# Loading K of head 6 and V of head 5 in one transfer each, with one TensorE loop for the V products of head 5, and c and x in four transfers

## The chip, the cores and the metric

The kernel runs on one core of one Trainium2 chip. The metric is the device time of one execution in microseconds (us). A core has five engines that run side by side: TensorE (PE, matrix products; PEld is its weight load), VectorE (DVE), ScalarE (ACT), GpSimd (POOL) and SyncE (SP), which issues most DMA transfers. All transfers of the core share 16 DMA engines.

## What is computed

One token is decoded through an adaptive-layernorm block. The modulation is `silu(c) @ w_mod`, cut into six vectors of 512. The attention has 32 query heads over 8 key/value heads of 32768 cached positions and 128 channels; the caches are nearly all of the bytes.

```python
h = _layernorm(x) * (1 + ca) + sa
q = (h @ wq)                       # 32 heads of 128
p = softmax(q . k * Dh ** -0.5)    # 4 query heads share one k, v
x = x + ga * ((p @ v) @ wo)
h = _layernorm(x) * (1 + cb) + sb
x = x + gb * (relu(h @ w1) @ w2)   # 512 -> 1792 -> 512
```

## The kernel before

**Storage.** K or V of one head is 8 MB: 128 partitions of 256 positions of 128 channels. SBUF holds three such slots (pool `ring`, line 80), taken in turn by: the weights w_mod and wq, K0, K1, V0, K2, V1, K3, V2, K4, V3, K5, V4, K6, V5, K7, V6, V7, and a last slot for wo, w1 and w2. A load can be issued when the last reader of what lay three places earlier in that list is done. So V5 takes the slot of K5, K7 that of V4, V6 that of K6, V7 that of V5, and the last slot is that of K7.

**The stream.** The list `stream` (lines 161 to 168) fixes the order of the transfers, and all of them go through SP (line 154), in that order. K and V come whole (8 MB) for the early heads, and in halves (two of four steps, 4 MB) where `g >= HALVED`, with `HALVED = 5`: K6 and V5 in halves one after the other, then K7 and V6 half by half in turn. V7 comes in three parts, and the second half of K0 in three (lines 136 to 141): nearly all of it, then the last 512 bytes of rows 0 to 110, then those of rows 111 to 127. A reader waits for the transfer that holds its part. Every transfer raises one of eight completion semaphores, given out in turn over all transfers, those of ACT included; a transfer is issued only when the one that used its semaphore before has landed.

**One head.** For head h, DVE turns K within 32x32 blocks in eight pieces (`turn_k`, line 439, 128x2048 each); PE multiplies each piece with the queries in 8 products (`scores`, line 458), 64 for a head. Then `softmax` runs (lines 466 to 510): a maximum on DVE (line 471), two small PE transposes (476, 490), the exponential on ACT (495), a turn of the result on DVE (500), and on PE the sum (506). The products with V of the head before, `pv(g)` with g = h - 1, are 64 matmuls (line 520).

**How the order around the change is set.** PE and DVE run in the order in which the program is written (`manual_schedule`, lines 633 to 792). For g from 0 to 5 it is: scores of head g + 1; if `g >= HALVED`, `pv(g, (0, 1))`; the softmax of head g + 1; the rest of `pv(g)`, with the sum of the softmax behind it. So for head 5, 32 of the 64 V products are written out ahead of the softmax of head 6 (and run from steps 0 and 1 of V5), and the other 32 behind it. For heads 0 to 4 all 64 stand behind it. The V products behind the softmax are a PE loop (lines 523 to 531) for heads 0 to 5; the 32 ahead of it, and all of heads 6 and 7, are written out. The loop is a critical section: it begins when all that is written before it is done, the exponential of the softmax included. DVE's first operation after a softmax is tied behind the loop's place in the program, and `reciprocal` (line 509), which needs the sum that follows the loop, stands on DVE between the first and the second four turns of the next K (for head 7: between the second and the third).

**The end.** After head 7's scores the last slot's transfers are issued, PE works off the V products of heads 6 and 7, the rows of wo (`project`), the layernorm, w1 (line 761) and w2 (line 784), and DVE closes (789, 791).

**The start.** c and x come by one ACT transfer each into 8 of the 16 partitions of `cx_row` (lines 180 to 182); DVE spreads them (246), and the modulation (322), the first layernorm and the queries (393 to 408) follow.

Of the kernel before, what the change touches and what calls it, by code (L numbers as in the profile page):

```python
# [17 lines left out]
def kernel(  # L18
# [14 lines left out]
    nc = tc.nc  # L33
# [14 lines left out]
    WOROWS = 2  # L48
    LAST = Hkv - 1
    LOOPED = Hkv - 2  # L50
    HALVED = LOOPED - 1
    W2P = [(0, 5), (5, 10), (10, 12), (12, 13), (13, 14)]
    W1P = [(0, KT)]

# [108 lines left out]
    for g in range(LOOPED):  # L163
        stream += [("k", g + 1, s) for s in (halves if g >= HALVED else whole)] + [("v", g, s) for s in (halves if g >= HALVED else whole)]
    for s in halves:
# [5 lines left out]
    def need(key):  # L171
        while key not in loaded:
            load(stream[pos[0]])
            pos[0] += 1
        return loaded[key]
# [3 lines left out]
    wm_sb = need(("wm",))  # L179
    cx_row = const.tile([16, D // 8], BF16)  # L180
    for i, row in enumerate((c[0], A_x[0, 0])):
        nc.scalar.dma_start(out=cx_row[8 * i:8 * i + 8], in_=row.rearrange("(a n) -> a n", a=8))

    ident_bf = const.tile([P, P], BF16)
    make_identity(nc, ident_bf[:])
# [9 lines left out]
    for hp in range(4):  # L195
# [10 lines left out]
        out=mask4, in_=ident_f[:].rearrange("p (x q) -> p q x", q=REP), op=ALU.add, axis=AX.X,  # L206
# [3 lines left out]
    for n in sorted({n * REP for _, n in WOP}):  # L210
        cmask[n] = const.tile([P, P // n], F32, name=f"cmask{n}")
        nc.vector.tensor_reduce(
            out=cmask[n][:], in_=ident_f[:].rearrange("p (c r) -> p c r", r=n), op=ALU.add, axis=AX.X,
# [3 lines left out]
            out=rsel_f[:], in_=ident_f[:].rearrange("p (c r) -> p r c", r=n), op=ALU.add, axis=AX.X,  # L217
# [6 lines left out]
        out=smask[:], in_=ident_f[0:16, 0:16].rearrange("p (s q) -> p s q", q=REP), op=ALU.add, axis=AX.X,  # L224
# [8 lines left out]
        out=place32[:], in_=ident_f[:].rearrange("p (j m) -> p m j", m=32), op=ALU.add, axis=AX.X,  # L233
# [4 lines left out]
        out=rowpick[:, OUT0:OUT1], in_=ident_f[:].rearrange("p (j m) -> p j m", m=32), op=ALU.add, axis=AX.X,  # L238
# [8 lines left out]
        out=cx_bd, in0=cx_row[:].unsqueeze(1).to_broadcast([16, 8, D // 8]),  # L247
# [112 lines left out]
    def four_rows(e, name):  # L360
# [16 lines left out]
        out=nca[:], in0=modT_sb[:, KT:2 * KT], scalar1=-1.0, scalar2=-1.0, op0=ALU.mult, op1=ALU.add,  # L377
# [3 lines left out]
        out=ncb[:], in0=modT_sb[:, 4 * KT:5 * KT], scalar1=-1.0, scalar2=-1.0, op0=ALU.mult, op1=ALU.add,  # L381
# [17 lines left out]
    for i in range(2):  # L399
        nc.vector.transpose(out=q_cols[:, i, :], in_=q_ps[i])  # L400
        nc.scalar.copy(
            out=qT_sb[:, 16 * i:16 * (i + 1)], in_=q_cols[:, i, :].rearrange("p (h r) -> p h r", r=32)[:, :, 0],
# [109 lines left out]
    def pv(g, us, js=range(16)):  # L512

        nb = 4 // len(us)

        PT_g = PT_tiles[g][:].rearrange("p (h j c) -> p h (j c)", h=2, c=32)
        Vs = [need(("v", g, u)) for u in us]

        def step(u, V, PT, Vx):
            nc.tensor.matmul(o_tiles[g][:], lhsT=PT, rhs=Vx, start=False, stop=False, skip_group_check=True)  # L520

        Vf = [V.rearrange("p (s j) d -> p s (j d)", s=4) for V in Vs]
        if g < HALVED or g == HALVED and us[0] > 0:

            with tc.tile_critical() as section:
                last_loop[:] = loop[:] = [section.name]
                with nc.tensor.Fori(0, 512 - 32 * nb + 1, 32 * nb) as at:
                    for b in range(nb):
                        for u, V in zip(us, Vf):
                            step(u, V, PT_g[:, u // 2, 32 * b + 16 * (u % 2):][:, bass.DynSlice(at, 16)],  # L530
                                 V[:, :, Dh * b:][:, :, bass.DynSlice(at * (Dh // 32), Dh)])
        else:
            for u, V in zip(us, Vf):
                for j in js:
                    c0 = 32 * j + 16 * (u % 2)
                    step(u, V, PT_g[:, u // 2, c0:c0 + 16], V[:, :, Dh * j:Dh * (j + 1)])
# [22 lines left out]
    def part_of(g):  # L559
        return [i for i, (g0, n) in enumerate(WOP) if g0 <= g < g0 + n][0]  # L560
# [17 lines left out]
    def spread(i):  # L578

        n = WOP[i][1] * REP  # L580
        o2_ps = small_ps([P, n], "o2_ps")
        nc.tensor.matmul(  # L582
            o2_ps[:], lhsT=oA[i][:].rearrange("p h c -> p (h c)"), rhs=rsel[n][:], start=True, stop=True,
        )
        o2 = const.tile([P, n], BF16, name=f"o2_sb{i}")
        nc.vector.tensor_copy(out=o2[:], in_=o2_ps[:])  # L586
        o2_tiles[i] = o2
# [45 lines left out]
    with tc.manual_schedule(engines={mybir.EngineType.PE, mybir.EngineType.DVE}):  # L633
# [9 lines left out]
        for g in range(LOOPED):  # L643
            h = g + 1
            build_qbd(h)
            for u in range(NTILE):
                for half in range(2):
                    turn_k(h, u, half)
                    scores(h, u, half)
                if soft and u == 1:  # L650
                    next(soft, None)
            if g - 1 in [sum(w) for w in WOP]:
                spread(part_of(g - 2))
            if g >= HALVED:
                pv(g, (0, 1))
            soft = softmax(h)
            next(soft)
            if g > 0:
                blocks(g - 1)
            next(soft)  # L660
            if g > 0:
                o_cols(g - 1)
            next(soft)
            next(soft)
            pv(g, (2, 3) if g >= HALVED else (0, 1, 2, 3))
            if g > 0:
                normalise(g - 1)
            next(soft)
            open_o(h)
            next(soft)  # L670
        g, h = LOOPED, LAST
# [13 lines left out]
        spread(part_of(g - 1))  # L685
        bank_max(h, 0)
        pv(g, (0, 1))
        for u in (2, 3):
            for half in range(2):
# [48 lines left out]
            out=x1T[:], in0=x1T[:], scalar=1.0, in1=xT, op0=ALU.mult, op1=ALU.add, accum_out=stat2[:, 0:1],  # L738
# [31 lines left out]
        for f0, f1 in ((0, FT // 2), (FT // 2, FT)):  # L770
            nc.vector.transpose(out=hidT[:, f0:f1], in_=hid_v[:, f0:f1])
            nc.scalar.activation(
                out=AP(hb.tensor, hb.offset + 32 * f0 + 31, [hb.ap[0], [32, f1 - f0]]),
                in_=hidT[:, f0:f1, 0], func=ACT.Relu,
            )

        for part, (f0, f1) in enumerate(W2P):
            w2_sb = need(("w2", part))
            for ft in range(f0, f1):
                for i in (0, 2, 1, 3):  # L780
                    row = OUT0 + i
# [41 lines left out]
```

## Time and profile before

| what | before |
|---|---|
| median of 3 runs | 354.26 us (354.23 to 354.55) |
| span of the profiled execution | 352.6 us |
| PE busy | 277.9 us, 79% |
| DVE busy | 201.0 us, 57% |
| ACT busy | 25.1 us, 7% |
| read from HBM | 149.42 MB, 424 GB/s over the span |
| granted TensorE clock, mean | 0.937 |

The profile is of one execution. The page gives its span, from the first to the last instruction, and no other time of it; the median of the runs is 1.66 us longer than this span. A page has the busy time of the engines, the span in 40 slices, the DMA queues, the chain of work that ended last, and groups of instructions by source line. The trace behind it can be asked for a timeline: each row is start, duration, engine, line, operation, tiles, count, and in brackets the idle time of the engine before it and what ended that. `DVE Ksb L439 ... <-DMA` means that DVE sat idle until a piece of K had landed. A loop's matmuls stand in one row with their count.

### The profile page before, as it was taken

The numbers are of one execution on the slowest core, as the hardware profiler recorded it, in microseconds if no ns is written. First come the engines' busy times: TensorE is split into PE (matmuls) and PEld (weight loads), VectorE is DVE, ScalarE is ACT, GpSimd is POOL, SyncE is SP. The second block draws the span as 40 slices with busy tenths as digits, with TensorE's granted clock in tenths as the row PEclk, the third lists the DMA queues.
The fourth block names the chain that finished last, engine by engine and source line by source line (L and its number), as shares of the span: only waits on it lengthen the run. The fifth ranks groups of instructions, "written<-read, shape, count | busy, mean of one in ns | idle before, by whom it ended". The sixth has DMA issues, their size and how long they took to land. (4 is left out here: it accounts for less than half of the span.)

```text
span 352.6 us, 3715 instructions
## 1 busy us (share of the span) xinstructions
PE 277.9 (79%) x1310; PEld 113.5 (32%) x1310; DVE 201.0 (57%) x226; ACT 25.1 (7%) x69; POOL 3.1 (1%) x15
## 2 busy tenths in 40 slices
PE   0065891895998599976998499968999799989994
PEld 0021330331333234322333134323444233434442
DVE  6663564984079614974099506975684257744142
ACT  1200103002000200001000200011000100011000
POOL 2000000000000000000000000000000000000000
PEclk9999897798999879998999879996999989999999
DMA  9999989999999999999999999999999999999995
GB/s 357 398 435 452 472 388 461 454 394 454 461 394 448 439 424 439 424 433 439 416 446 446 409 440 461 411 394 454 431 414 435 457 417 420 444 439 409 425 425 214
DMA packets 5224, 149.59 MB, mean 424 GB/s; under 512 B 604, under 2 KB 988, under 8 KB 1628
## 3 DMA queue, kind: packets, MB, share of 16 engines
q1 hardware_dynamic: 5180, 149.43, 98.5%
q8 instruction: 8, 0.13, 0.1%
q14 instruction: 4, 0.03, 0.0%
q10 hardware_dynamic: 32, 0.00, 0.0%
HBM read 149.42 MB, written 0.00 MB: 424 GB/s over the span
## 5 line engine op out<-in xcount | busy, mean ns | idle before, releaser
L439 DVE STREAM_TRANSPOSE Ksb<-Ksb 128x2048 f32<-128x2048 f32 x60 | 133.1, 2276 | 60.2 <-DMA Ksb<-in_A_k_cache_dram 60.2
L520 PE MATMUL o_ps<-Vsb,P_g 128*16 (+1 forms) x512 | 127.0, 408 | 13.0 <-ACT P_g L495 10.0
L458 PE MATMUL S_ps<-Ksb,qbd 128*128 128x512 bf16 x512 | 120.4, 386 | 10.9 <-DVE Ksb L439 9.3
L458 PEld LDWEIGHTS <-qbd 128*128 128x128 bf16 x512 | 49.6, 98 | 78.1 <-issue 21.8
L520 PEld LDWEIGHTS o_ps<-Vsb,P_g 128*16 x352 | 34.0, 97 | 67.8 <-issue 36.5
L520 PEld LDWEIGHTS <-P_g 128*16 128x16 bf16 x160 | 13.8, 90 | 19.0 <-issue 0.4
L420 ACT COPY qbd<-qrep_sb 32x16 bf16<-32x16 bf16 x32 | 6.4, 201 | 175.2 <-PE S_ps L458 174.1
L500 DVE STREAM_TRANSPOSE P_g<-P_g 128x1024 bf16<-128x1024 bf16 x8 | 10.0, 1245 | 14.1 <-ACT P_g L495 14.1
L471 DVE TENSOR_REDUCE m_p<-S_ps 128x1 f32<-128x1024 f32 x7 | 8.6, 1223 | 13.3 <-PE S_ps L458 13.3
L322 PE MATMUL mod_ps<-wmq_sb,siluT 128*1 128x512 bf16 x24 | 3.6, 624 | 9.9 <-DMA wmq_sb<-in_w_mod_dram 9.9
L331 DVE STREAM_TRANSPOSE Ksb<-Ksb 128x2048 f32<-128x2048 f32 x4 | 8.9, 2280 | 1.6 <-DMA Ksb<-in_A_k_cache_dram 1.6
L476 PE MATMUL mT_ps<-ident_f,m_p 128*1 128x128 f32 x8 | 2.2, 270 | 8.9 <-DVE m_p L471 7.9
L495 ACT ACTIVATE P_g<-S_ps,nbias 128x1024 bf16<-128x1024 f32 x8 | 8.9, 1114 | 0.2
L506 PE MATMUL L_ps<-Lexp,ones_f 128*128 128x4 f32 x16 | 3.1, 263 | 6.3 <-DVE Lexp L503 4.3
L492 ACT ACTIVATE nbias<-Mb_ps 128x1 f32<-128x1 f32 x8 | 1.4, 171 | 88.3 <-PE Mb_ps L490 88.3
L509 DVE RECIPROCAL Linv<-L_ps 128x4 f32<-128x4 f32 x8 | 1.3, 164 | 10.9 <-PE L_ps L506 10.9
L252 PE MATMUL xc_ps<-cx_sel,wmq_sb 16*128 16x2 bf16 x4 | 0.3, 172 | 8.7 <-DVE wmq_sb L246 8.7
L555 PE MATMUL acc_ps<-mask_sb,Y 16*128 16x4 f32 x16 | 3.0, 258 | 4.9 <-DVE Y L551 4.9
L548 DVE TENSOR_TENSOR o_ps<-o_ps,smask 16x512 f32<-16x512 f32 x8 | 5.3, 668 | 2.8 <-PE o_ps L520 2.8
L586 DVE CAST o_sb<-o_ps 128x4 bf16<-128x4 f32 (+2 forms) x4 | 0.7, 165 | 10.3 <-PE o_ps L582 10.3
L506 PEld LDWEIGHTS L_ps<-Lexp,ones_f 128*128 128x128 f32 x16 | 2.6, 203 | 9.6 <-issue 5.6
L551 DVE TENSOR_REDUCE Y<-o_ps 16x128 f32<-16x512 f32 x8 | 5.4, 678 | 0.3
(116 smaller groups left out, 82.8 us busy)
## 6 DMA issues: line engine op xcount, KB each, us to landing
Ksb<-in_A_k_cache_dram SPq DMA_DIRECT2D x5, 4096.0 KB, 23.5
Vsb<-in_A_v_cache_dram SPq DMA_DIRECT2D x5, 4096.0 KB, 38.0
wmq_sb<-in_A_wq_dram SPq DMA_DIRECT2D x1, 4096.0 KB, 28.0
Vsb<-in_A_v_cache_dram SPq DMA_DIRECT2D x2, 2048.0 KB, 38.1
Ksb<-in_A_k_cache_dram SPq DMA_DIRECT2D x1, 4032.0 KB, 37.1
wmq_sb<-in_w_mod_dram SPq DMA_DIRECT2D x1, 3072.0 KB, 18.8
tail_sb<-in_A_wo_dram SPq DMA_DIRECT2D x1, 2048.0 KB, 23.0
tail_sb<-in_B_w_dram SPq DMA_DIRECT2D x1, 1792.0 KB, 30.4
```

The costliest lines, as they stand in the source:

```text
L322: nc.tensor.matmul(dst[j // 4][32 * (j % 4):32 * (j % 4) + 1, :], lhsT=src_T[:, kt:kt + 1], rhs=w[:, kt, j * 512:(j + 1) * 512], start=(kt ...
L331: nc.vector.transpose(out=t, in_=t)
L420: nc.scalar.copy(out=o, in_=i)
L439: t = nc.vector.transpose(out=KTt.bitcast(F32), in_=KTt.bitcast(F32))
L458: nc.tensor.matmul(S_ps_tiles[g], lhsT=qbd[g % 2][:, hp, 4 * (7 - s):4 * (7 - s) + P], rhs=KTv[:, 16 * sl:16 * sl + 16, h, :, par], start= ...
L471: behind_loop(nc.vector.reduce_max(out=m_p[:], in_=S_g.rearrange("p g f -> p (g f)"), axis=AX.X))
L495: nc.scalar.activation(out=P_g[:], in_=S_g.rearrange("p g f -> p (g f)"), func=ACT.Exp, bias=nbias[:], scale=scale, accum_out=l_g[:],)
L500: behind_loop(nc.vector.transpose(out=P_g[:], in_=P_g[:]))
L506: nc.tensor.matmul(L_ps[:], lhsT=ones_f[:], rhs=Lexp[:], start=True, stop=True)
L520: nc.tensor.matmul(o_tiles[g][:], lhsT=PT, rhs=Vx, start=False, stop=False, skip_group_check=True)
L548: nc.vector.tensor_tensor(out=o, in0=o, in1=smask[:].unsqueeze(2).to_broadcast([16, 4, Dh]), op=ALU.mult,)
L551: nc.vector.tensor_reduce(out=Y[:], in_=o.rearrange("p s d -> p d s"), op=ALU.add, axis=AX.X)
```

## The change

K of head 6 and V of head 5 are each loaded by one transfer of 8 MB in place of two of 4 MB; the order of the bytes stays. All 64 V products of head 5 are one PE loop behind the softmax of head 6, as for heads 0 to 4. c and x come by two ACT transfers of four partitions each. In the built program the transfers of K7 and of all that follow have the same semaphores as before, since two are added at the start and two are taken away later; 32 matmuls and their 32 weight loads leave the written-out part of PE. After it all line numbers from 183 on are higher by one.

```diff
-    HALVED = LOOPED - 1
+    HALVED = LOOPED
...
     for i, row in enumerate((c[0], A_x[0, 0])):
-        nc.scalar.dma_start(out=cx_row[8 * i:8 * i + 8], in_=row.rearrange("(a n) -> a n", a=8))
+        for a in (8 * i, 8 * i + 4):
+            nc.scalar.dma_start(out=cx_row[a:a + 4], in_=row.rearrange("(a n) -> a n", a=8)[a % 8:a % 8 + 4])
...
-        if g < HALVED or g == HALVED and us[0] > 0:
+        if g < HALVED:
```

## The prediction

> **What bounds the kernel now.** I read the page first: the DMA row, the transfers' total, and the chain that ended last.
>
> ```profile
> DMA  9999989999999999999999999999999999999995
> DMA packets 5224, 149.59 MB, mean 424 GB/s; under 512 B 604, under 2 KB 988, under 8 KB 1628
> DMA 19%; PE 5%; DVE 3%; SPq 0%; issue 0%
> ```
>
> The 16 DMA engines are never idle before the last slice, and the chain ends in transfers. So the stream of bytes sets the end, unless PE comes late to the last weights. The bytes and their order stay, so I ask two things of the change: does the queue run dry anywhere, and how late does PE become? For the first I read SP's timeline, which tells when transfers are issued.
>
> ```profile
> 218.05 0.80 SPq L154 DMA_DIRECT2D Ksb<-in_A_k_cache_dram  x2
> ...
> 256.12 0.33 SPq L154 DMA_DIRECT2D Ksb<-in_A_k_cache_dram  x1
> 270.62 0.33 SPq L154 DMA_DIRECT2D Vsb<-in_A_v_cache_dram  x1
> ...
> 271.46 19.78 SPq L154 DMA_DIRECT2D Vsb<-in_A_v_cache_dram  x4
> 313.02 1.75 SPq L154 DMA_DIRECT2D tail_sb<-in_A_wo_dram  x4
> ```
>
> K6 is issued at 218.05, K7's first half at 256.12, V6's at 270.62; the row from 271.46 ends with the three parts of V7 near 291, and the tail follows at 313.02. For the second I read the timeline of heads 5 and 6, DVE and PE.
>
> ```profile
> 214.63 8.89 DVE L439 STREAM_TRANSPOSE Ksb<-Ksb 128x2048 f32<-128x2048 f32 x4 [12.14 <-DMA Ksb<-in_A_k_cache_dram]
> ...
> 234.35 1.22 DVE L471 TENSOR_REDUCE m_p<-S_ps 128x1 f32<-128x1024 f32 x1 [1.99 <-PE S_ps L458]
> ...
> 239.65 16.31 PE L520 MATMUL o_ps<-Vsb,P_g 128*16 x64 [2.04 <-ACT P_g L495]
> ...
> 243.75 8.89 DVE L439 STREAM_TRANSPOSE Ksb<-Ksb 128x2048 f32<-128x2048 f32 x4 [2.73 <-DMA Ksb<-in_A_k_cache_dram]
> ...
> 256.30 0.36 PE L506 MATMUL L_ps<-Lexp,ones_f 128*128 128x4 f32 x2 [0.34 <-PEq L525]
> ...
> 256.51 14.07 PE L458 MATMUL S_ps<-Ksb,qbd 128*128 128x512 bf16 x64
> ...
> 270.53 7.07 PE L520 MATMUL o_ps<-Vsb,P_g 128*16 128x512 bf16 x32
> 270.75 1.21 DVE L471 TENSOR_REDUCE m_p<-S_ps 128x1 f32<-128x1024 f32 x1
> ...
> 280.74 9.03 PE L520 MATMUL o_ps<-Vsb,P_g 128*16 x32 [2.10 <-DMA Ksb<-in_A_k_cache_dram]
> ...
> 290.10 0.36 PE L506 MATMUL L_ps<-Lexp,ones_f 128*128 128x4 f32 x2 [0.34 <-PEq L525]
> ```
>
> Head 5 is the pattern of a whole K: DVE idles 12.14 us for the landing at 214.6, turns eight pieces, and the maximum starts at 234.35, 19.72 us after the landing. Head 6 is the pattern of halves: DVE starts at 243.75 on the first half, while PE is still in the loop of head 4 that ends at 256.30. So PE does the 64 scores without a wait in 14.07 us, and 32 V products of head 5 (7.07 us) lie over the softmax of head 6.
>
> **The change, part by part.**
>
> *K6 whole.* Its first four pieces must wait for the second half. No row shows that landing, since nobody waits for it; an estimate comes from the rows at 243.75 and at 302.15 (below), where DVE waits for the first half of K6 and the second of K7: six halves in 58.4 us, 9.73 each, so K6 is in at 253.5. By head 5's pattern head 6's maximum then starts at 253.5 + 19.7 = 273.2, plus 0.1 for the small copy that stands before it here: 273.3. Before: 270.75. Queued behind the waiting turn on DVE are the other turns and head 5's reciprocal, whose reader comes much later; the scores wait for the turns. **Term one: 2.5 us.**
>
> *All V products of head 5 behind the softmax.* From the maximum to the loop of 64 takes 239.65 - 234.35 = 5.30 us, from the loop's start to the sum behind it 256.30 - 239.65 = 16.65: 21.95 in all. Before, the same way took 290.10 - 270.75 = 19.35. **Term two: 2.6 us.** The sum of head 6 moves from 290.10 to 273.3 + 21.95 = 295.2, **5.1 us later**. The 64 products may take other times:
>
> ```profile
> 84.24 17.68 PE L520 MATMUL o_ps<-Vsb,P_g 128*16 x64 [2.02 <-ACT P_g L495]
> ```
>
> This loop took 17.68 where that at 239.65 took 16.31, so up to 1.4 more; twice the written-out 7.07 gives 14.1, so up to 2.2 less. I take the nearest, the loop just before.
>
> *The way to the end.*
>
> ```profile
> 298.57 7.07 PE L520 MATMUL o_ps<-Vsb,P_g 128*16 128x512 bf16 x32
> 298.76 0.68 DVE L464 TENSOR_REDUCE m<-S_ps 128x1 f32<-128x512 f32 x1
> 302.15 8.89 DVE L439 STREAM_TRANSPOSE Ksb<-Ksb 128x2048 f32<-128x2048 f32 x4 [2.70 <-DMA Ksb<-in_A_k_cache_dram]
> 305.58 7.41 PE L458 MATMUL S_ps<-Ksb,qbd 128*128 128x512 bf16 x32
> ...
> 332.70 3.62 PE L520 MATMUL o_ps<-Vsb,P_g 128*16 128x512 bf16 x16
> ...
> 336.02 1.16 PE L595 MATMUL end_ps<-tail_sb,o_sb 128*1 128x512 bf16 x16
> ...
> 343.70 0.22 DVE L305 SCALAR_TENSOR_TENSOR h2T<-cen_ln,rstd_ln,modT_sb 128x4 bf16<-128x4 f32 x1
> ...
> 345.30 0.93 PE L761 MATMUL hid_ps<-tail_sb,h2T 128*1 128x448 bf16 x16 [1.28 <-DMA tail_sb<-in_B_w_dram]
> ...
> 347.07 0.73 PE L784 MATMUL end_ps<-tail_sb 128*32 128x128 bf16 x20
> 348.32 1.58 PE L784 MATMUL end_ps<-tail_sb 128*32 128x128 bf16 x36 [0.52 <-DMA tail_sb<-in_B_w_dram]
> ```
>
> The V products at 298.57 stand 8.47 us behind the sum and wait for nothing of the stream, so they start at 303.7. DVE's maximum at 298.76 moves to 303.9, and the last four turns, which began with the landing at 302.15, begin at 304.5 and end at 313.4. PE comes to those scores at 303.7 + 7.0 = 310.7 and does all 32 in 7.1, to 317.8; its last eight start near 316, after the turns. Before they ended at 312.99. **PE is 4.8 us late at the end of the scores**, since 0.3 us of its waiting for DVE goes.
>
> From there PE had no pause for a transfer before 336, where the first rows of wo came as the V products ended (332.70 + 3.62 = 336.32), so the 4.8 us stay. They meet three waits for the stream: 1.28 us ahead of w1 (345.30), 0.52 ahead of w2's second piece (348.32), and, in the last 36 products, what they take beyond the pace of the 20 before them, 1.58 - 36 x 0.73/20 = 0.27. The lateness eats **2.1 us**. What is late next is PE alone; the layernorm's result, ready at 343.92, sets the start of w1 in place of the transfer. **4.8 - 2.1 = 2.7 us later.**
>
> *The queue.* V6's first half, issued at the end of head 6's scores, moves from 270.62 to about 273.2; K7's first half, issued at 256.12 as before, feeds the engines until 253.5 + 3 x 9.73 = 282.7, which leaves 9 us. V7 moves from near 290 to 295.2, and is due when six halves behind K6 (V5, K7, V6) are in, at 311.9: 17 us. The tail moves from 313.02 to 317.8, due after V7 at 331: 13 us. So these moves cost nothing; with cover gone, each would cost its own 2.6 to 5.1 us. The queue behind the issuing SP holds only these transfers in this order. The two saved issues are 0.4 us of SP each (0.80 for two at 218.05), while it has nothing else to do.
>
> *Boundaries.* The Trainium skill's page "DMA: Bandwidth & Descriptors" (Anatomy of one DMA) gives each transfer about 2.0 us beside its bytes, which speaks for this change. The rows here have it hidden behind the next transfer: half a V or K takes 9.73, and two are 19.46. Head 4's and head 5's K, with one whole V between, land at
>
> ```profile
> 176.10 8.89 DVE L439 STREAM_TRANSPOSE Ksb<-Ksb 128x2048 f32<-128x2048 f32 x4 [12.24 <-DMA Ksb<-in_A_k_cache_dram]
> ```
>
> and 214.63, so 19.27 for a whole one. I take 0 for a boundary, the bounds being 0 and 0.2 us.
>
> *c and x, and the start.*
>
> ```profile
> 2.12 20.99 SPq L154 DMA_DIRECT2D Ksb<-in_A_k_cache_dram  x4
> 7.99 0.68 DVE L246 TENSOR_TENSOR wmq_sb<-cx_row,pick 16x512 bf16<-16x512 bf16 x1 [1.82 <-DMA cx_row<-in_A_x_dram]
> 12.76 8.89 DVE L331 STREAM_TRANSPOSE Ksb<-Ksb 128x2048 f32<-128x2048 f32 x4 [1.63 <-DMA Ksb<-in_A_k_cache_dram]
> 20.05 3.58 PE L322 MATMUL mod_ps<-wmq_sb,siluT 128*1 128x512 bf16 x24 [9.86 <-DMA wmq_sb<-in_w_mod_dram]
> 35.10 0.35 SPq L154 DMA_DIRECT2D Vsb<-in_A_v_cache_dram  x1
> 60.18 6.70 DVE L439 STREAM_TRANSPOSE Ksb<-Ksb 128x2048 f32<-128x2048 f32 x3 [0.62 <-DMA Ksb<-in_A_k_cache_dram]
> ```
>
> x was there at 7.99. Two more small transfers add between nothing and twice that, to 24. PE's first large work waits 9.86 us for w_mod anyway; beyond that, V0's issue at 35.10 could slip by 25 us until K1 is in at 60.18. Two semaphores fewer at the start make K0's last small piece wait for K0's first landing, near 12.7, and K1 queues behind it on SP; K1's bytes come last in a queue that lasts until about 41 (60.18 less a whole transfer). Zero for both, and each later head starts anew at its own landing (12.14 us of DVE idle at 214.63).
>
> **Sum.** The profiled execution has a span of 352.6 us; the median of the runs, 354.26, is 1.66 more, which I take for what lies around the span. 352.6 + 2.7 + 1.66 = **357.0 us**, 0.8% slower. A measurement of this kernel can tell about 0.2%, 0.7 us, from no change.
>
> **The rivals.**
>
> *Only one of the two terms arises* (8%): if head 6's scores did not wait for the whole K, or the softmax were covered otherwise, PE would be 2.2 to 2.3 us late against 2.1 of cover: +0.2, **354.4**, no change. Against it: one transfer has one landing that everyone waits for, and the loop at 239.65 began only behind ACT's exponential, as its bracket says.
>
> *The stream shortens* (5%, the other side): each removed boundary saves b, so K6 lands b earlier and the stream ends 2b earlier. The end moves by the later of 2.7 - b (PE) and -2b (stream): faster from b = 2.7 us on, below 351. The 0.2 us above speaks against it. I give b above 2.7 us 3%, and a b of some 2 us, with PE's lateness still deciding, 2%. By the figure of the page "DMA: Bandwidth & Descriptors" of the Trainium skill, 2.0 us for b, the end would move by +0.7, to 355.0; no row here shows it.
>
> *A slow loop* (10%): PE idles ahead of the 64 products, and they run like those at 84.24: +1.4, **358.4**. The loop of head 4 at 239.65, behind the same pause, did not.
>
> **How the numbers follow.** Forecast 77%: 356 to 358. The range reaches from 355.5 (cover larger by half, or the loop shorter by 1.5) to 358.6 (slow loop, landing 0.2 later). Below it lie the rivals of one term and of the shorter stream, 13% together; the sign follows: slower 0.89 (forecast, slow loop, small b), within 0.2% 0.08, faster 0.03.
>
> **What would show it.** In the changed profile: DVE's wait for K6 ends near 253.5, not 243.7; the maximum of head 6 starts near 273; a loop of 64 starts near 278.6 and the sum follows near 295; head 7's scores end near 318; no DMA row below 9 before the end; w1's products wait for DVE, not DMA. Wrong: a slice of the DMA row that drops near 282 or 312 (a dry queue), PE waiting for w1 as before (cover too small in my sum), or K6 turning before 250.

## The result and the profile after

The changed kernel takes 357.11 us (median of 6) against 354.38 for the kernel before: ratio 1.0077, 95% interval 1.0066 to 1.0088. One of the six, 366.65 us at a granted clock of 0.92, was in a slower state that the kernel before also shows in some runs, and such runs are left out of every ratio. The span of the profiled execution is 355.1 us, 2.5 more. From the page after, the DMA row, the rate in GB/s of the 40 slices, and the chain that ended last:

```profile
DMA  8999999999999999999999999999998999999992
GB/s 355 409 429 456 450 422 436 436 436 428 436 443 423 436 458 406 443 452 407 436 458 406 436 458 406 430 458 413 436 450 382 447 437 417 443 430 415 424 419 93
PE 13%; DVE 3%; issue 0%; ACT 0%; ACTq 0%
```

The stream is as full as before. The one 8 late in the row is the slice from 266 to 275 us with 382 GB/s; its neighbours have 450 and 447, 426 in the mean of the three, and the next wait for a landing below (282.34) ends no later than the same one before:

```profile
282.51 4.51 DVE L439 STREAM_TRANSPOSE Ksb<-Ksb 128x2048 f32<-128x2048 f32 x2 [0.46 <-DMA Ksb<-in_A_k_cache_dram]
```

So this is no dry queue. The chain, 19% DMA before, has no DMA in it any more: PE and DVE set the end.

The timeline after, with the rows that answer to those of before (lines are one higher):

```profile
12.94 0.68 DVE L247 TENSOR_TENSOR wmq_sb<-cx_row,pick 16x512 bf16<-16x512 bf16 x1 [6.77 <-DMA cx_row<-in_A_x_dram]
...
35.40 0.35 SPq L154 DMA_DIRECT2D Vsb<-in_A_v_cache_dram  x1
...
253.38 8.89 DVE L440 STREAM_TRANSPOSE Ksb<-Ksb 128x2048 f32<-128x2048 f32 x4 [12.29 <-DMA Ksb<-in_A_k_cache_dram]
...
273.23 1.21 DVE L472 TENSOR_REDUCE m_p<-S_ps 128x1 f32<-128x1024 f32 x1
...
278.46 16.09 PE L521 MATMUL o_ps<-Vsb,P_g 128*16 x64 [2.00 <-ACT P_g L496]
...
282.34 4.51 DVE L440 STREAM_TRANSPOSE Ksb<-Ksb 128x2048 f32<-128x2048 f32 x2 [2.46 <-DMA Ksb<-in_A_k_cache_dram]
294.90 0.36 PE L507 MATMUL L_ps<-Lexp,ones_f 128*128 128x4 f32 x2 [0.34 <-PEq L526]
...
304.15 8.88 DVE L440 STREAM_TRANSPOSE Ksb<-Ksb 128x2048 f32<-128x2048 f32 x4
...
310.37 7.12 PE L459 MATMUL S_ps<-Ksb,qbd 128*128 128x512 bf16 x32
317.52 1.75 SPq L154 DMA_DIRECT2D tail_sb<-in_A_wo_dram  x4
...
348.12 0.22 DVE L306 SCALAR_TENSOR_TENSOR h2T<-cen_ln,rstd_ln,modT_sb 128x4 bf16<-128x4 f32 x1
...
348.40 0.93 PE L762 MATMUL hid_ps<-tail_sb,h2T 128*1 128x448 bf16 x16
...
350.16 1.74 PE L785 MATMUL end_ps<-tail_sb 128*32 128x128 bf16 x56
...
352.57 0.29 SPq L793 DMA_DIRECT2D out_dram<-o_bf  x1
```

Head 6 now waits for its landing like head 5: DVE idles 12.29 us, until 253.38. The maximum comes at 273.23 (before 270.75), the 64 products follow the softmax, and the sum stands at 294.90 (before 290.10). DVE turns the last pieces of K7 without a wait for a landing, and the products with w1 and w2 have no wait for a transfer in their brackets: the 20 and 36 with w2, which were apart before, are one row of 56. The output was issued in the kernel before at

```profile
350.57 0.29 SPq L792 DMA_DIRECT2D out_dram<-o_bf  x1
```

so it comes 2.00 us later, while the span grew by 2.5 (and the median by 2.73, over several executions). The half microsecond behind the output's issue is in no step of the prediction.

### The profile page after: what moved, and what is told of

Its sections match the earlier page's. It is cut to its first block, busy times and chain, and to the rows that moved or that the text cites. A ratio compares the mean times of both kernels' runs of the same rounds, so it can differ in the third digit from the quotient of the medians.

```text
span 355.1 us, 3754 instructions
## 1 busy us (share of the span) xinstructions
PE 278.9 (79%) x1310; PEld 113.4 (32%) x1310; DVE 200.5 (56%) x226; ACT 25.1 (7%) x69; POOL 3.1 (1%) x15
## 5 line engine op out<-in xcount | busy, mean ns | idle before, releaser
L459 PE MATMUL S_ps<-Ksb,qbd 128*128 128x512 bf16 x512 | 121.9, 387 | 12.1 <-DVE Ksb L440 8.1
L521 PEld LDWEIGHTS o_ps<-Vsb,P_g 128*16 x384 | 36.6, 95 | 71.5 <-issue 38.4
L521 PEld LDWEIGHTS <-P_g 128*16 128x16 bf16 x128 | 11.0, 90 | 15.0 <-issue 0.2
L556 PEld LDWEIGHTS acc_ps<-mask_sb,Y 16*128 16x128 f32 x16 | 2.7, 214 | 8.4 <-DVE Y L552 7.9
```

The costliest lines, as they stand in the source:

```text
L459: nc.tensor.matmul(S_ps_tiles[g], lhsT=qbd[g % 2][:, hp, 4 * (7 - s):4 * (7 - s) + P], rhs=KTv[:, 16 * sl:16 * sl + 16, h, :, par], start= ...
L556: nc.tensor.matmul(oT_ps, lhsT=Y_tiles.pop(g)[:], rhs=qsel, start=True, stop=True, skip_group_check=True,)
```

## The experiments

The theory: PE gets late by two terms, K6's single landing and V products that no longer lie over the softmax, and the waits for the stream at the end eat about 2 us of it. Each ratio below is to runs of the kernel before on the same chip; its interval is 95%.

### 1. c and x alone

```diff
-        nc.scalar.dma_start(out=cx_row[8 * i:8 * i + 8], ...)
+        for a in (8 * i, 8 * i + 4):
+            nc.scalar.dma_start(out=cx_row[a:a + 4], ...)
```

in the kernel before. 

> The kernel before with one part of the change alone: c and x in four transfers. Theory (PE late by two terms, 2.5 us from K6's single landing and 2.6 us from V products that no longer lie over the softmax, against some 2.1 us of waits at the end that eat lateness): the start is covered, so 354.4 us, ratio 1.000 within 0.001. Rival start (the split or the eight semaphores cost the 2.7 us): 357.1, ratio 1.0077. Profile: the spread of c and x on DVE starts near 13 instead of 8 us, and head 7's scores end near 313 as before.

Measured: 355.19 us, ratio 1.0023 (1.0013 to 1.0032). Neither theory has this. The tail of its timeline, with its span from its page:

```profile
350.90 0.29 SPq L793 DMA_DIRECT2D out_dram<-o_bf  x1
```

```profile
span 353.6 us, 3718 instructions
```

The spread of c and x starts at 13.00, and the tail's transfers, issued behind head 7's scores, start at 313.35, as expected. The output's issue is 0.33 us later in this execution, which took 0.23 more than the median. But 2.74 us lie between the issue and the end of the span, against 2.03 in the kernel before: 0.7 of the 0.76 us by which the medians differ. So the start is covered, as priced, and the close is not the same. Experiments 9, 10 and 12 take this up.

### 2. The whole change without c and x

The changed kernel with the two transfers of c and x as before. 

> The changed kernel with c and x back in two transfers. Theory: 357.1 us, ratio 1.0077 as the whole change. Rival start: 354.4, ratio 1.000.

Measured: 357.35 us, ratio 1.0082 (1.0068 to 1.0096). The start as the whole cost is out. The profiled execution was the slowest of the five (358.14): its loop took 16.83 us at a mean granted clock of 0.83, where that of the changed kernel took 16.09 at 0.91, and its output was issued at 353.55.

### 3. The V products alone

```diff
-        if g < HALVED or g == HALVED and us[0] > 0:
+        if g < LOOPED:
...
-            if g >= HALVED:
-                pv(g, (0, 1))
...
-            pv(g, (2, 3) if g >= HALVED else (0, 1, 2, 3))
+            pv(g, (0, 1, 2, 3))
```

in the kernel before; all loads stay. 

> The kernel before with one part alone: all 64 V products of head 5 in one loop behind the softmax; K6, V5, c and x are loaded as before. Theory: the sum behind the loop starts near 292.7 instead of 290.1, head 7's scores end near 315.3, PE is 2.3 us late and 2.1 to 2.5 of that is eaten: 354.4 to 354.7, ratio 1.000 to 1.001. Rival additive (each term moves the end by its own share, nothing is eaten twice): +1.4 us, 355.8, ratio 1.004. Rival loop (the products' loop is the whole cost): 357.1.

Measured: 354.47 us, ratio 1.0002 (0.9993 to 1.0011). Its timeline:

```profile
275.88 16.83 PE L520 MATMUL o_ps<-Vsb,P_g 128*16 x64 [1.99 <-ACT P_g L495]
...
293.05 0.36 PE L506 MATMUL L_ps<-Lexp,ones_f 128*128 128x4 f32 x2 [0.34 <-PEq L525]
...
346.28 0.22 DVE L305 SCALAR_TENSOR_TENSOR h2T<-cen_ln,rstd_ln,modT_sb 128x4 bf16<-128x4 f32 x1
...
350.74 0.29 SPq L790 DMA_DIRECT2D out_dram<-o_bf  x1
```

The sum is 2.95 us later than in the kernel before, the layernorm's result still 2.58, the output 0.17. The lateness is there and is eaten. Additive costs (355.8) are out.

### 4. K6 whole, alone

```diff
-        stream += [("k", g + 1, s) for s in (halves if g >= HALVED else whole)] + ...
+        stream += [("k", g + 1, s) for s in whole] + ...
```

in the kernel before; V5 stays in halves, its first 32 products over the softmax. 

> The kernel before with one part alone: K of head 6 in one transfer; V of head 5 in halves, 32 of its products over the softmax as before, c and x in two transfers. Theory: head 6's maximum starts near 273.2 instead of 270.75, head 7's scores end near 315.2, PE is 2.2 us late and all of it is eaten: 354.4 to 354.6, ratio 1.000 to 1.001. Rival additive: +1.3 us, 355.7, ratio 1.004. Rival queue (the large transfer holds the queue and is the whole cost): 357.1, with a DMA slice below 9.

Measured: 354.75 us, ratio 1.0010 (1.0001 to 1.0019). Its timeline:

```profile
273.18 1.21 DVE L471 TENSOR_REDUCE m_p<-S_ps 128x1 f32<-128x1024 f32 x1
...
281.31 1.11 ACT L495 ACTIVATE P_g<-S_ps,nbias 128x1024 bf16<-128x1024 f32 x1
...
282.36 8.74 PE L520 MATMUL o_ps<-Vsb,P_g 128*16 x32 [1.29 <-DMA Ksb<-in_A_k_cache_dram]
...
291.44 0.35 PE L506 MATMUL L_ps<-Lexp,ones_f 128*128 128x4 f32 x2 [0.34 <-PEq L525]
...
350.44 0.29 SPq L792 DMA_DIRECT2D out_dram<-o_bf  x1
```

The maximum is 2.4 us late, as expected. The sum is only 1.3 late: the loop started 9.2 us behind the maximum, not 10.0 as in the kernel before, and ran 0.3 us shorter. It did not wait for the exponential, which ended at 282.42, after the loop's start. In the kernel before, the exponential is

```profile
278.88 1.11 ACT L495 ACTIVATE P_g<-S_ps,nbias 128x1024 bf16<-128x1024 f32 x1
```

and the loop, at 280.74, started 0.75 us behind its end. Why this wait is absent here was not tried. So this run tests the first term only in part: PE is 1.05 us late at the end of head 7's scores, not the 2.2 expected. The output is not late at all (350.44). The 0.3 us of the median are in the close again: the span is 353.0 us, 2.5 behind the output's issue. The queue as the cause (357.1) is out.

So each of these two parts alone moves the output's issue by 0.2 us or less, and both together by 2.00: the terms are paid only where their sum exceeds the cover. V5's single transfer was not tried by itself; after the change the loop that reads V5 waits for ACT (278.46), not for a transfer.

### 5 and 6. The cover by itself

```diff
         blocks(g)
+        keep_clock(10)        # 20 in the second
         pv(LAST, (0, 1))
```

in the kernel before. An idle product is one whose result nothing reads. Ten took 2.32 us on PE, twenty 4.48. 

> The kernel before with 10 idle 512-column products put on PE ahead of head 7's first V products (about 0.215 us each, 2.15 us in all); nothing else differs, no transfer is touched. It measures the cover by itself. Theory: lateness of 2.15 us is eaten by the waits of the tail: 354.4 to 354.6, ratio 1.000 to 1.001. Rival no cover (the tail follows PE one for one): 356.5, ratio 1.006.

Measured: 354.39 us, ratio 0.9997 (0.9988 to 1.0006). 

> The kernel before with 20 such idle products (4.3 us). Theory: 4.3 less a cover of 2.1 to 2.5: +1.8 to +2.2 us, 356.2 to 356.6, ratio 1.005 to 1.006, close to the changed kernel though no transfer and no loop was touched. Rival no cover: 358.7, ratio 1.012. Rival large cover: 354.4.

Measured: 356.26 us, ratio 1.0049 (1.0035 to 1.0063). The timeline with twenty:

```profile
321.56 4.48 PE L631 MATMUL spare_ps<-qbd,ident_bf 128*128 128x512 bf16 x20
325.96 7.07 PE L520 MATMUL o_ps<-Vsb,P_g 128*16 128x512 bf16 x32
...
348.15 0.93 PE L762 MATMUL hid_ps<-tail_sb,h2T 128*1 128x448 bf16 x16
349.91 1.74 PE L785 MATMUL end_ps<-tail_sb 128*32 128x128 bf16 x56
...
352.32 0.29 SPq L793 DMA_DIRECT2D out_dram<-o_bf  x1
```

With no transfer and no loop touched, the tail looks like that of the changed kernel: no bracket at w1, 56 products in one row, the output 1.75 us late. The V products behind the idle ones started in the kernel before at

```profile
321.73 7.07 PE L520 MATMUL o_ps<-Vsb,P_g 128*16 128x512 bf16 x32
```

so PE is 325.96 - 321.73 = 4.23 us late there; the cover is 4.23 - 1.75 = 2.5 us.

### 7. The products of the changed kernel written out

```diff
-        if g < HALVED:
+        if g < HALVED - 1:
```

in the changed kernel: no loop for head 5. 

> The changed kernel with the 64 V products of head 5 written out behind the softmax instead of a loop. Theory: the loop waits for ACT's exponential, written-out products only for PE's own small transposes, so they start about 2 us sooner, near 276.4; the sum follows near 292.5, PE is about 2.1 us late at the end of head 7's scores, and that is eaten: 354.4 to 354.8, ratio 1.000 to 1.001. Rival (where the products stand matters, not what they wait for): 357.1.

Measured: 355.05 us, ratio 1.0016 (1.0007 to 1.0025). Most of the change's cost goes, but the size was missed by some 0.3 us. Its timeline:

```profile
276.60 16.92 PE L521 MATMUL o_ps<-Vsb,P_g 128*16 128x512 bf16 x64
293.45 0.39 PE L507 MATMUL L_ps<-Lexp,ones_f 128*128 128x4 f32 x2
```

They start 1.9 us sooner than the loop, as expected: no wait for the exponential. But they took 16.92 us, and the sum came at 293.45, not 292.5. Two things that the expectation lacked explain the miss. The close is 2.51 us here, 0.5 more than in the kernel before. And the length of the row differs between executions: in the profile of experiment 11, the same products with a short close,

```profile
276.62 15.67 PE L521 MATMUL o_ps<-Vsb,P_g 128*16 128x512 bf16 x64
```

at a mean granted clock of 0.89, against 0.82 here.

### 8. Lateness added to the changed kernel

The same ten products in the changed kernel. 

> The changed kernel with the 10 idle products of about 2.15 us in all ahead of head 7's first V products. Theory: no cover is left, so the end follows one for one: 357.1 + 2.15 = 359.25, ratio 1.0137. Rival (the transfers still set the end of the changed kernel): 357.1 to 357.5.

Measured: 359.23 us, ratio 1.0135 (1.0120 to 1.0151), 2.12 over the changed kernel, one for one. In the kernel before the same ten cost nothing (5). No cover is left after the change.

The profiles of all these kernels give the cover once more. PE's lateness is read where the tail's transfers are issued, behind head 7's scores (313.02 in the kernel before), and the output's at its issue (350.57):

| kernel | PE late, us | output late, us | difference, us |
|---|---|---|---|
| 4 | 1.05 | -0.13 | 1.18 |
| 11 | 1.85 | 0.11 | 1.74 |
| 3 | 2.66 | 0.17 | 2.49 |
| 7 | 3.08 | 0.58 | 2.50 |
| after | 4.50 | 2.00 | 2.50 |
| 2 | 5.48 | 2.98 | 2.50 |

Lateness up to about 2.5 us is eaten, and all beyond it comes out at the end.

### 9, 10, 11 and 12. The close

SP's records in the traces show a pause of 0.43 us ahead of its 80th instruction (0.43 to 0.46 from the start of the 79th to that of the 80th), whether that is a wait for a semaphore or a drain. Its place against the output's issue differs with how many instructions SP has before. "Close" is the time from the output's issue to the span's end:

| kernel | SP's instructions ahead of the output's issue | close, us |
|---|---|---|
| before, 5, 6 | 75 | 2.02 to 2.03 |
| 3 | 74 | 2.03 |
| 4 | 73 | 2.53 |
| after, 7, 8 | 71 | 2.51 |
| 2 | 71 | 2.69 |
| 1 | 75 | 2.74 |

With 74 or 75 the pause falls ahead of the wait for the output's landing, which ends 1.2 us behind its issue: in the kernel before the pause lies from 0.51 to 0.93 us behind the issue. With 71 or 73 it falls behind that wait: after the change from 1.26 to 1.68. With c and x alone (1) the pause has the place of before, but the output has another of the eight semaphores and is waited for first, so the pause comes behind that wait. In 2 the output also has another semaphore, and two more waits of SP stand behind its landing than in the changed kernel, which adds 0.18. The number of drains (SP instructions that do no work there) behind V0's issue (`SPACE`, line 58, 14) shifts the count where SP has nothing to do:

```diff
-    SPACE = 14
+    SPACE = 18        # 9, changed kernel; 10 in experiment 10, 18 in 11, 22 in 12
```

> The changed kernel with four more drains on SP behind V0's issue (18 in place of 14), where SP has nothing to do. In all ten profiles so far SP pauses some 0.43 to 0.46 us ahead of its 80th instruction; in the kernel before that lies over the landing of the output, in the changed one, whose SP has four instructions fewer, behind it, and the time from the output's issue to the end of the span is 2.52 us against 2.03. Theory of the pause: with the count restored the close is 2.03 again, the time 356.6 us, ratio 1.0062. Rival (the longer close belongs to the later end itself): 357.1, ratio 1.0077, close 2.5.

Measured: 356.59 us, ratio 1.0060 (1.0046 to 1.0074), close 2.03.

> The kernel before with four drains fewer on SP (10 in place of 14), nothing else. Theory of the pause: it moves behind the output's landing, the close grows from 2.03 to about 2.5 us, the time to 354.9, ratio 1.0013. Rival: 354.4, close 2.03.

Measured: 354.95 us, ratio 1.0016 (1.0007 to 1.0025), close 2.52. Four drains that do nothing are worth half a microsecond.

> The changed kernel with head 5's V products written out behind the softmax and 18 drains. Theory: PE's lateness is nearly eaten (the last sum on DVE came 0.6 us later than in the kernel before), and the close is short again: 354.5 to 354.7 us, ratio 1.000 to 1.001. Rival (the 0.55 us of the written-out kernel are PE's alone): 355.0, ratio 1.0016.

Measured: 354.51 us, ratio 1.0002 (0.9993 to 1.0011), close 2.02.

> The kernel before with c and x in four transfers and 22 drains on SP. In c and x alone the close was 2.75 us: the first wait of the close took 0.85 us, since the output has another of the eight semaphores there and is waited for first, and the pause of 0.45 came behind it. Theory: with eight more SP instructions the pause lies ahead of the output's issue, the close is about 2.3 us, the time 354.7, ratio 1.0008 to 1.001. Rival (the start costs it): 355.2, ratio 1.0023.

Measured: 354.71 us, ratio 1.0007 (0.9999 to 1.0016), close 2.30. From the pages and timelines of 9 and 10, span and output's issue:

```profile
span 354.6 us, 3758 instructions
```

```profile
352.60 0.29 SPq L793 DMA_DIRECT2D out_dram<-o_bf  x1
```

```profile
span 353.2 us, 3711 instructions
```

```profile
350.65 0.29 SPq L792 DMA_DIRECT2D out_dram<-o_bf  x1
```

In 9 the output is issued when it was in the changed kernel (352.57), and the span still ends half a microsecond sooner. The theory of the pause holds in all four; in 12 the pause itself can't be seen, since SP waits there for a transfer anyway. What the pause is was not tried; its place by count, and not by time or by what the instruction does, is what the other 13 profiles show. With count and products both set right (11), the changed loads and c and x cost nothing that these runs can tell. No version here beats the kernel before.

## Why the prediction was right

*The total was right, and partly because two misses cancel.* PE's lateness less its cover was to be 4.8 - 2.1 = 2.7 us. It was 4.5 - 2.5 = 2.0, and 0.5 of close, which the prediction did not have, came on top. Experiment 9 separates them: 356.59 without the 0.5. The mechanism was right, and that the total came within 0.1 us of the forecast was luck.

*Term one*, 2.5 us: right. K6 was in at 253.38 (estimated 253.5) and the maximum 2.48 us late.

*Term two*, 2.6 us: right in cause (experiment 3 alone made the sum 2.95 us late, with a loop of 16.83; in the changed kernel the loop took 16.09). In the changed kernel the sum was 4.8 us late, not 5.1: 273.23 to 294.90 is 21.67, not 21.95. Part of the loops' difference is in the granted clock: mean 0.91 over the loop after, 0.83 over that of experiment 3.

```profile
278.40:294.90 16.50, 16.09 (x65) 5.96 (x65) 5.90 (x5) 0.00 (x0) 0.00 (x0) 0.91 1.00 429
```

```profile
275.80:293.05 17.25, 16.83 (x64) 6.39 (x65) 5.91 (x5) 0.00 (x0) 0.00 (x0) 0.83 1.01 437
```

These are busy times of PE, PEld, DVE, ACT and POOL in the stretch, then the clock. The Trainium skill's page "TensorE: Matmul & The Clock Gate" (Part 1: The HAM clock gate) says that the window by which the clock is raised runs free, so that the count of slow products differs from run to run. These two loops agree with it: both follow a stretch of over 5 us in which PE has only a few small products, and their clock differs; so do the rows of 7 and 11, 16.92 us at 0.82 and 15.67 at 0.89.

*The way to the end*: right. The tail's transfers were issued at 317.52 (predicted 317.8), 4.5 us late; DVE's last turns were no longer tied to a landing.

*The cover* was 0.4 us too small. w1's start moved by 348.40 - 345.30 = 3.10, so 1.4 of 4.5 went there, near the 1.28 counted. The mis-sized term is w2: 56 products took 1.74 us in one go, where they had taken from 347.07 to 349.90, so 1.1 went there and not 0.79. The pace taken from the row of 20 (0.73) holds the tail of its last product, which the long row pays once. Experiment 6 and the table behind 8 give 2.5 us in all.

*The queue, boundaries*: right. V6's, V7's and the tail's later issues left no gap, and K6 landed when its two halves would have; nothing like the 2 us of the Trainium skill's page "DMA: Bandwidth & Descriptors" (Anatomy of one DMA) was saved, as the rows of before said. That page of the Trainium skill fits its figure on transfers issued from GpSimd, while SP issues these. The DMA row's 9 stands for 90% or more, and one slice before has an 8, so "never idle" says somewhat more than the row.

*c and x, the start*: right for the start. c and x were spread at 12.94 in place of 7.99, inside the bounds of 8 to 24, and V0 was issued 0.3 us later. But "zero for both" overlooked what else a change of the number of transfers touches: SP's instruction count and which semaphore the output has. Alone, the split costs 0.2% through the close (1, 12).

*The rivals*: "only one of the two terms" described experiments 3 and 4 well: 354.4 was its time, 354.47 and 354.75 theirs, the latter with 0.5 of close. The shorter stream did not come; its "below 351" does not follow from its own sum either, by which a b of 3 us moves the end by 2.7 - 3 = -0.3, to 354.0. A loop as slow as 17.68 us did not come; the slowest was 16.83, in 3 and in the profile of 2.

## What to carry to other kernels

Price a delay on an engine off the critical path against the sum of the waits that end last behind it: here 2.5 us were free, so either of the two parts alone moved the output by 0.2 us at most and both together by 2.0. Read a bracket that vanishes and rows that merge (20 and 36 products into 56) as cover used up. Before a difference of a few tenths of a per cent is put down to the work, compare the time from the last output's issue to the end of the span.

## What the runs showed of the hardware

SP paused 0.43 us ahead of its 80th instruction in 13 of the 14 profiles (in that of 12 it waits there anyway), so four empty SP instructions far from the end moved the time by 0.5 us (experiments 9 and 10). Splitting the two small transfers of c and x into four, 2 KB in all and issued on ACT within the first 2.3 us, made the last of them usable 5 us later beside the large ones (7.99 to 12.94; with the split alone 13.00, with the rest of the change alone 7.95).
